# A long convolution's inverse transform: u times D added in PSUM by an identity matmul, the odd classes' second sums on GpSimd, and one rotation pass for both halves

## The chip, the core and the metric

The kernel runs on one core of a Trainium2 chip. The core has a matrix engine (TensorE, PE in the rows; PEld is its weight load), a vector engine (VectorE, DVE), a scalar engine (ScalarE, ACT), GpSimd (POOL) and a queue engine (SyncE, SP) that here only issues DMAs. Each engine works through a queue of its own in order; semaphores make one wait for another. The metric is device time in microseconds, the median of several runs.

## The reference, cut to what matters

Two independent parts are computed and joined along the last axis. Part A is attention over 64 segments of 32 tokens, with eight memory tokens carried from each segment to the next, so that segments follow one another. Part B is a state-space layer: a convolution kernel K of length 2048 per channel from 128 complex states, applied to u (2048 x 1024) by an FFT of length 4096, and u times a vector D added:

```python
P = jnp.exp(logdA[:, :, None] * l[None, None, :])
K = jnp.einsum('dn,dnl,dn->dl', Cc, P, dB).real
...
Yf = Uf * Kf[None, :, :, :]
y = irfft2(Yf, ...).astype(jnp.bfloat16)[:, :, 0, :L]
y = transpose(y, 0, 2, 1) + u * Dskip[None, None, :]
```

## The kernel before

The program runs part B first, then part A. Part B (`part_b`, from L709) has two stages. The first, up to about 400 us, builds the tables and transforms u; it leaves the transform of u in DRAM (`Ud`, f32), the rows that give the spectrum of K, and the matrices of the inverse transform (`MId`). The second, which the change edits, is called the Transform here: the loop `for b in range(16)` at L1547 and the tail behind it.

The loop's iteration b is one of four blocks of frequencies (`kc = b % 4`) of one of four quarters of the channels (`dq = b // 4`, 256 channels each). A block has two halves (`n_`), each with two sub-blocks and a real and an imaginary part: 128 x 1024 numbers in f32. Within an iteration:

- PE forms the spectrum of K for iteration b + 1 (`spectrum`, L1214, products at L1221, 20 for each half) into PSUM (`hps`, three buffers; `pa` in the first iterations).
- DVE multiplies it by the transform of u (`times_u`, L1374): `Z` and `Y` at L1377, one operand in SBUF (`wq`, the loaded `Ud`), one in PSUM. `rotate` (L1379) makes a complex product of them in two half-size passes, L1380 and L1381. The first half is rotated before the second half's products; the second half after the u work of the iteration.
- `pointwise` (L1443) then adds and subtracts the halves on DVE: the sum (`even`, tile `ev`, f32) at L1456, the difference straight into the bf16 operand `Bt[:, kc, 1]` at L1457. GpSimd makes the even classes' two second sums from `even` (L1459, 512 wide each). There is no second sum for the odd classes.
- From iteration 4 on, PE computes two inverse products (`inverses(2)`) for the quarter that was finished before. An output block is a pair of row blocks c of class r = c // 4; the eight pairs are taken in the order `PAIRS = (0, 4, 2, 6, 8, 12, 10, 14)`, so that each iteration has one even and one odd class. `products_back` (L1500, products at L1511) runs over two row blocks, four kc and two parts: 16 products for an even class; for an odd class 32, as it reads both sub-blocks of the difference, the second through matrices whose sign ACT has turned (`negated`, L1470, tile `mn`, L1474). Some pairs get one more small product (L1506).
- ACT scales the result out of PSUM into bf16 (`yb`, L1526). `ending` (L1530) multiplies the u rows by D on DVE (L1531) and adds `yb` (L1532); the write to DRAM is issued on ACT's queue (L1533). These endings are run by `end()` in the next iteration, between the second half's products and its rotation.

SP's queue carries everything that is loaded, in an order that the program fixes: in each iteration the two halves of `Ud` for the next one (L1212, each waits until DVE has used the old one), then between none and three weight blocks for part A of 512 KB (`residents`, L1682; the load is L268), each into a place that part B has given up, and then the u rows for later inverse products (`load_inverse`, L1464, three ahead, seven buffers `uu`). Iteration 6 also loads the second set of K's rows (L1095), on which the spectrum of iteration 8 depends.

After the loop three inverse products of the last quarter are begun in the `hps` banks (`begun`, L1603) with the first three kc, and the last eight inverses run, with nine weight loads after the first and one after each other. Then part A starts: DVE copies the first kept weights through PSUM into `arena` (L335), PE runs the projections (L414) and the output products (L527), and weights that don't fit are streamed again in every segment (`wst`).

Of the kernel before, what the change touches and what calls it, by code (L numbers as in the profile page):

```python
# [708 lines left out]
def part_b(ctx, tc, u, A_re, A_im, B_re, B_im, C_re, C_im, log_dt, Dskip, out_b, ahead, copies, residents, first_state):  # L709
# [732 lines left out]

    def pointwise(b, s_):  # L1443
        kc, Bt = b % 4, Bs[b // 4]
        Y = first
        if b:
            Y = pw.tile([128, 2, 2, 2, DQ], F32, name="y", tag="y")[:]
            for n_ in range(2):
                Z = pw.tile([128, 2, 2, DQ], F32, name="z", tag="z")[:]
                times_u(s_, Y[:, n_], Z, n_)  # L1450
                if n_ == 0:
                    rotate(Y[:, n_], Z)
        yield
        if b:
            rotate(Y[:, 1], Z)
        v.tensor_tensor(out=even[:], in0=Y[:, 0], in1=Y[:, 1], op=ALU.add)  # L1456
        v.tensor_tensor(out=Bt[:, kc, 1], in0=Y[:, 0], in1=Y[:, 1], op=ALU.subtract)  # L1457
        for i, op in ((0, ALU.add), (1, ALU.subtract)):
            gp.tensor_tensor(out=Bt[:, kc, 0, i], in0=even[:, 0], in1=even[:, 1], op=op)  # L1459

    NIV, UU = 3, 7
    unsent = []

    def load_inverse(dq, c):  # L1464
        r, mc = c // 4, c % 4
        uu = iv.tile([128, 2, DQ], BF16, name="uu", tag="uu", bufs=UU)
        sy.dma_start(out=uu[:], in_=u_v[r][:, mc:mc + 2, DQ * dq:DQ * dq + DQ])
        return uu

    def negated(c):  # L1470
        cs, mn = (None, 1, None, 0)[c // 4], None
        if cs is not None:
            mn = mnp.tile([128, 2, 4, 128], BF16, name="mn", tag="mn")
            sc.activation(out=mn[:], in_=MI[c // 2][:, :, cs], func=ACT.Copy, scale=-1.0)  # L1474
        return cs, mn

    ready = []

    def inverses(n):

        for _ in range(n):
            dq, c = todo.pop(0)
            if not ready:
                ready.append(negated(c))
            inverse(dq, c, nxt.pop(0), *ready.pop(0))
            if len(todo) >= NIV:
                nxt.append(load_inverse(*todo[NIV - 1]))
# [3 lines left out]
    def prepare(n):  # L1491
        while len(ready) < min(n, len(todo)):
            ready.append(negated(todo[len(ready)][1]))

    def inverse_begin(dq, c, yp):
        prepare(3)
        early[dq, c] = yp
        products_back(yp, dq, c, *ready[PAIRS.index(c)], range(3))

    def products_back(yp, dq, c, neg, mn, kcs):  # L1500
        r, Bt = c // 4, Bs[dq]
        j = r % 2
        for b in range(2):
            for kc in kcs:
                if kc == 3 and b == 1 and c % 4 == 2:
                    pe.matmul(yp[:, b, :], lhsT=l4[:, r, :], rhs=w4[:, DQ * dq:DQ * dq + DQ], start=False, stop=False, skip_group_check=True)  # L1506
                for cs in range(2):
                    hs = (0, 1) if j else (r // 2,)
                    for half in hs:
                        lhs = mn[:, b] if j and half and cs == neg else MI[c // 2][:, b, cs]  # L1510
                        pe.matmul(yp[:, b, :], lhsT=lhs[:, kc, :], rhs=Bt[:, kc, j, half, 1 - cs if j and half else cs, :],  # L1511
                                  start=(b == 0 and kc == 0 and cs == 0 and half == hs[0]), stop=(kc == 3 and cs == 1 and half == hs[-1]),
                                  skip_group_check=True)

    def inverse(dq, c, uu, neg, mn):
        r, mc = c // 4, c % 4
        d = slice(DQ * dq, DQ * dq + DQ)
        if (dq, c) in early:
            yp = early[dq, c]
            products_back(yp, dq, c, neg, mn, range(3, 4))  # L1520
        else:
            yp = ps_y.tile([128, 2, DQ], F32, name="yp", tag="yp")[:]
            products_back(yp, dq, c, neg, mn, range(4))
        prepare(2)
        yb = iv.tile([128, 2, DQ], BF16, name="yb", tag="yb", bufs=2)
# [3 lines left out]

        def ending():  # L1530
# [246 lines left out]
```

## Time and profile before

| What | Value |
|---|---|
| median of three runs | 1961.17 us (1948.34, 1961.17, 1962.83) |
| profiled execution, its own time | 1945.78 us |
| span of the profiled execution | 1944.1 us |
| mean granted TensorE clock | 0.976 |
| loop of the Transform, first product of iteration 4 to that of iteration 15 | 446.35 to 575.22 us |
| first product of part A on PE | 607.84 us |

A row of a timeline has the start and the length in us, the engine, the line, the operation, the tile written and the tiles read, shapes (partitions x elements) and a count of merged instructions; a bracket at its end gives how long the engine had stood idle and what ended the wait. Adjacent rows of one engine overlap a little, so the pitch from start to start is the cost of one. A row of windows gives a stretch, then its length, the busy time of PE, PEld, DVE, ACT and POOL with the number of instructions, the granted clock, the share of time that the DMA engines were busy, and GB/s. A row of waits gives who waited for whom: the total, the number of times and the longest.

### The profile page before, as it was taken

How to read it: one execution, taken by the hardware profiler on the slowest of the kernel's cores; microseconds unless marked ns; L12 is line 12 of the kernel's file. 1: busy time of each engine (PE TensorE's matmuls, PEld its weight loads, DVE VectorE, ACT ScalarE, POOL GpSimd, SP SyncE). 2: the span in 40 equal slices, each digit the busy share in tenths (PEclk: the TensorE clock that was granted, in tenths of full speed). 3: DMA queues.
4: the chain of work that ended last, by engine and by line, in shares of the span. 5: the costliest groups of instructions: out<-in, count | busy, mean ns of one | idle time of the engine just before them, and what ended most of it. 6: DMA issues, size and time to landing. Idle time of an engine off the chain costs nothing.

```text
span 1944.1 us, 74320 instructions
## 1 busy us (share of the span) xinstructions
PE 1802.1 (93%) x31750; PEld 1115.6 (57%) x31788; DVE 1370.7 (71%) x3431; ACT 935.6 (48%) x1670; POOL 459.2 (24%) x855
## 2 busy tenths in 40 slices
PE   8999999887997899998999999999999999999998
PEld 3666566556775455555555555555555555555554
DVE  8699999789893566666676666666666666666650
ACT  8799999851112344443444444444434443434330
POOL 2363545223222111111121111111111111111120
PEclk9999999869998999999999999999999999999999
DMA  7889898867589999999999999999999999999990
GB/s 223 248 237 270 253 285 244 217 190 254 169 264 322 349 337 349 348 350 321 349 349 345 346 347 345 344 340 348 339 333 357 352 343 342 340 345 353 342 348 27
DMA packets 337343, 591.09 MB, mean 304 GB/s; under 512 B 94848, under 2 KB 211048, under 8 KB 334964
## 3 DMA queue, kind: packets, MB, share of 16 engines
q1 hardware_dynamic: 284824, 531.85, 80.2%
q10 hardware_dynamic: 45532, 29.57, 5.0%
q0 software_dynamic: 6656, 24.92, 3.5%
q8 instruction: 249, 4.08, 0.8%
q14 instruction: 82, 0.67, 0.1%
HBM read 528.78 MB, written 68.47 MB: 307 GB/s over the span
## 4 chain that ended last, share of the span: by engine, by line
PE 39%; DMA 27%; DVE 2%; ACT 1%; issue 1%; SPq 0%; POOL 0%; ACTq 0%; POOLq 0%; DVEq 0%
PE acc L414 22%; DMA wst<-WD_v 11%; DMA wst<-WD_o 9%; PE pp L527 9%; PE pe L664 3%; PE tr L425 2%; DMA wst<-WD_k 2%; DMA arena<-PKd 2%; PE pv L495 1%; DMA wst<-WD_q 1%; DMA out_dram<-arena 1%; DVE arena L621 1%; PE pv L499 1%; ACT arena L621 1%; DMA out_dram<-uu 1%
## 5 line engine op out<-in xcount | busy, mean ns | idle before, releaser
L414 PEld LDWEIGHTS <-a_hT 128*32 128x32 bf16 x12352 | 329.4, 96 | 324.0 <-issue 64.6
L420 ACT CAST arena<-acc 128x512 bf16<-128x512 f32 x384 | 225.1, 586 | 389.5 <-PE acc L414 316.3
L414 PE MATMUL acc<-wst,a_hT 128*32 128x512 bf16 x2304 | 230.4, 383 | 33.0 <-DMA wst<-WD_v 26.1
L527 PEld LDWEIGHTS <-arena 128*32 128x32 bf16 x8256 | 216.2, 97 | 77.0 <-issue 53.0
L428 POOL COPY arena<-arena 128x128 bf16<-128x128 bf16 x128 | 37.4, 292 | 697.3 <-PE tr L425 352.4
L335 DVE TENSOR_SCALAR arena<-keep 128x256 int32<-128x256 int32 (+1 forms) x512 | 175.6, 395 | 27.7 <-PE acc L414 27.5
L414 PE MATMUL acc<-XM,a_hT 128*32 128x512 bf16 x2560 | 173.0, 381 | 0.0
L454 DVE TENSOR_REDUCE a_mx<-sc 128x4 f32<-128x160 f32 (+1 forms) x192 | 71.8, 374 | 74.0 <-PE sc L442 74.0
L197 PE MATMUL pro<-XM,wsl 128*128 128x512 bf16 x480 | 117.7, 382 | 5.4 <-DVE kst L206 2.2
L527 PE MATMUL pp<-W_o,arena 128*32 128x256 bf16 x3584 | 120.7, 273 | 0.4 <-issue 0.4
L414 PE MATMUL acc<-W,a_hT 128*32 128x512 bf16 x1536 | 119.7, 384 | 0.0
L542 DVE COPY arena<-tr 128x512 bf16<-128x512 bf16 x64 | 27.2, 425 | 127.1 <-PE tr L425 127.1
L458 ACT ACTIVATE sc<-sc 128x160 f32<-128x160 f32 (+1 forms) x192 | 63.9, 333 | 105.1 <-DVE sc L455 104.8
L462 DVE TENSOR_REDUCE a_mx<-sc 128x4 f32<-128x160 f32 (+1 forms) x192 | 72.8, 379 | 55.3 <-ACT sc L458 55.1
L489 POOL TENSOR_TENSOR arena<-arena,a_BD 128x128 bf16<-128x128 bf16 x128 | 51.0, 399 | 218.0 <-DVE arena L472 213.2
L1266 DVE TENSOR_SCALAR nr<-ptt 128x456 f32<-128x456 int16 x128 | 80.4, 628 | 30.5 <-PE ptt L1244 27.5
L1258 ACT ACTIVATE E<-pa 128x648 bf16<-128x648 f32 x128 | 87.6, 712 | 17.1 <-PE pa L1250 15.5
L527 PE MATMUL pp<-wst,arena 128*32 128x256 bf16 x1536 | 76.4, 274 | 17.6 <-DMA wst<-WD_o 16.7
L414 PE MATMUL acc<-wq,a_hT 128*32 128x512 bf16 x1024 | 92.4, 383 | 0.0
L513 ACT CAST arena<-pv 128x512 bf16<-128x512 f32 (+1 forms) x128 | 61.3, 479 | 63.5 <-PE pv L499 33.1
L1459 POOL TENSOR_TENSOR Bt<-ev 128x512 bf16<-128x512 f32 x32 | 55.7, 1762 | 151.5 <-DVE ev L1456 151.5
L414 PE MATMUL acc<-g,a_hT 128*32 128x512 bf16 x1024 | 90.9, 381 | 0.0
(339 smaller groups left out, 4023.9 us busy)
## 6 DMA issues: line engine op xcount, KB each, us to landing
wst<-WD_v SPq DMA_DIRECT2D x256, 512.0 KB
wst<-WD_k SPq DMA_DIRECT2D x192, 512.0 KB
wst<-WD_o SPq DMA_DIRECT2D x192, 512.0 KB
wst<-WD_q SPq DMA_DIRECT2D x128, 512.0 KB
Ud<-ux POOLq DMA_DIRECT2D x16, 1024.0 KB, 8.4
wq<-Ud SPq DMA_DIRECT2D x32, 512.0 KB
wsl<-in_A_Wk_dram SPq DMA_DIRECT2D x16, 512.0 KB
wsl<-in_A_Wv_dram SPq DMA_DIRECT2D x16, 512.0 KB
```

The source lines that it names most:

```text
L197: nc.tensor.matmul(a[:], lhsT=w[:, kc, 128 * j:128 * j + 128], rhs=xTl[:, kc, :, :].rearrange("p s k -> p (s k)"), start=(kc == 0), stop=( ...
L335: nc.vector.tensor_scalar(out=out.bitcast(I32), in0=in_.bitcast(I32), scalar1=0, scalar2=None, op0=ALU.bitwise_or)
L414: nc.tensor.matmul(a[32 * g:32 * g + 32, o_:o_ + rhs.shape[1]], lhsT=hT[:, kc, :], rhs=rhs, start=(kc == 0), stop=(kc == KC - 1), tile_pos ...
L420: nc.scalar.copy(out=q, in_=a[:])
L454: nc.vector.tensor_reduce(out=m_, in_=x, axis=AX.X, op=ALU.max)
L458: nc.scalar.activation(out=flat(sc, i), in_=flat(sc, i), func=ACT.Exp, scale=scale)
L462: nc.vector.tensor_reduce(out=m_, in_=x, axis=AX.X, op=ALU.add)
L513: copy(out=o[:, i:i + n], in_=p[:, i:i + n, :].rearrange("p a (g q) -> p a g q", g=4))
L527: nc.tensor.matmul(po[32 * qt:32 * qt + 32, o_:o_ + rhs.shape[1]], lhsT=oT[:, h % 4, (h % 16) // 4, :], rhs=rhs, start=False, stop=(h == 3 ...
L664: nc.tensor.matmul(pe[n][:], lhsT=left[2 * b + hi // 16][:, 128 * (hi % 16):128 * (hi % 16) + 128], rhs=wo[u][:, 1024 * hh + 512 * n:1024 ...
L1258: sc.activation(out=T["E", r, e // 4][:, lo:lo + 8 * NE].rearrange("p (i c) -> p i c", i=2), in_=T.pop(("p", r, e))[:, :, 0:4 * NE], func= ...
L1266: v.tensor_scalar(out=T["n", r, e // 4][:, lo:lo + 8 * NT], in0=T.pop(("t", r, e))[:, 0:8 * NT].bitcast(I16)[:, 0:16 * NT:2], scalar1=floa ...
```

## The change

`Y` and `Z` become one tile each for both halves (`Yp`, `Zs`), and `even` is laid into the second half of `Zs`. From iteration 4 on both halves are rotated together, after the iteration's u work, in two passes of 128 x 1024; before that each half is rotated alone, as it was. The difference is written in f32 (`odd`), and GpSimd makes from it the two second sums of the odd classes, reading one operand with its halves in reversed order; in iteration 15 DVE makes these two. So an odd class needs 16 products, as an even one, and the negated matrices go, with ACT's work on them. The u rows are loaded in pairs into one tile (three buffers of two); one DVE pass (`skips`) multiplies a pair by D, before the inverse product that needs it, and PE adds the rows to the sum in PSUM with an identity matrix that has been scaled once by PLEN / 2 (a matmul of 512 columns per inverse). ACT's scaled copy `yb` (three buffers, two before) is then the result itself, written from there; the write of one inverse is issued after the copy of the next, no longer after a DVE sum.

```diff
-    mnp = ctx.enter_context(tc.tile_pool(name="b_mn", bufs=2))
     evp = ctx.enter_context(tc.tile_pool(name="b_ev", bufs=1))
-    even = evp.tile([128, 2, 2, DQ], F32, name="ev")
+    odd = evp.tile([128, 2, 2, DQ], F32, name="od")
...
+    Zs = pw.tile([128, 2, 2, 2, DQ], F32, name="z")
+    Yp = pw.tile([128, 2, 2, 2, DQ], F32, name="y")
+    even = Zs[:, 1]
+
+    def blocks(t_):
+        return t_.rearrange("p i c d -> p (i c) d")
+
     def pointwise(b, s_):
         kc, Bt = b % 4, Bs[b // 4]
-        Y = first
+        Y = Yp[:] if b else first
+        whole = b > 3
         if b:
-            Y = pw.tile([128, 2, 2, 2, DQ], F32, name="y", tag="y")[:]
             for n_ in range(2):
-                Z = pw.tile([128, 2, 2, DQ], F32, name="z", tag="z")[:]
-                times_u(s_, Y[:, n_], Z, n_)
-                if n_ == 0:
-                    rotate(Y[:, n_], Z)
+                times_u(s_, Y[:, n_], Zs[:, n_], n_)
+                if n_ == 0 and not whole:
+                    rotate(Y[:, n_], Zs[:, n_])
         yield
-        if b:
-            rotate(Y[:, 1], Z)
-        v.tensor_tensor(out=even[:], in0=Y[:, 0], in1=Y[:, 1], op=ALU.add)
-        v.tensor_tensor(out=Bt[:, kc, 1], in0=Y[:, 0], in1=Y[:, 1], op=ALU.subtract)
+        if whole:
+            rotate(Y.rearrange("p n a c d -> p (n a) c d"), Zs[:].rearrange("p n a c d -> p (n a) c d"))
+        elif b:
+            rotate(Y[:, 1], Zs[:, 1])
+        v.tensor_tensor(out=even, in0=Y[:, 0], in1=Y[:, 1], op=ALU.add)
+        v.tensor_tensor(out=odd[:], in0=Y[:, 0], in1=Y[:, 1], op=ALU.subtract)
         for i, op in ((0, ALU.add), (1, ALU.subtract)):
             gp.tensor_tensor(out=Bt[:, kc, 0, i], in0=even[:, 0], in1=even[:, 1], op=op)
-
-    NIV, UU = 3, 7
+        eng, to = v if b == 15 else gp, blocks(Bt[:, kc, 1])
+        eng.tensor_tensor(out=to[:, 0:4:3], in0=odd[:, 0], in1=odd[:, 1, ::-1], op=ALU.add)
+        eng.tensor_tensor(out=to[:, 2:0:-1], in0=odd[:, 0], in1=odd[:, 1, ::-1], op=ALU.subtract)
...
     def load_inverse(dq, c):
         r, mc = c // 4, c % 4
-        uu = iv.tile([128, 2, DQ], BF16, name="uu", tag="uu", bufs=UU)
-        sy.dma_start(out=uu[:], in_=u_v[r][:, mc:mc + 2, DQ * dq:DQ * dq + DQ])
+        i = turn_of[0] % 2
+        turn_of[0] += 1
+        if i == 0:
+            pairs.append(iv.tile([128, 2, 2, DQ], BF16, name="uu", tag="uu", bufs=3))
+        uu = pairs[-1][:, i]
+        sy.dma_start(out=uu, in_=u_v[r][:, mc:mc + 2, DQ * dq:DQ * dq + DQ])
         return uu
...
+    def skips():
+        dq = todo[0][0]
+        uu = pairs.pop(0)
+        d = slice(DQ * dq, DQ * dq + DQ)
+        uu = uu[:].rearrange("p i a d -> p (i a) d")
+        v.tensor_tensor(out=uu, in0=uu, in1=Dsk[:, d].unsqueeze(1).to_broadcast([128, 4, DQ]), op=ALU.mult)
...
                 for cs in range(2):
-                    hs = (0, 1) if j else (r // 2,)
-                    for half in hs:
-                        lhs = mn[:, b] if j and half and cs == neg else MI[c // 2][:, b, cs]
-                        pe.matmul(yp[:, b, :], lhsT=lhs[:, kc, :], rhs=Bt[:, kc, j, half, 1 - cs if j and half else cs, :],
...
+                    pe.matmul(yp[:, b, :], lhsT=MI[c // 2][:, b, cs, kc, :], rhs=Bt[:, kc, r % 2, r // 2, cs, :],
+                              start=(b == 0 and kc == 0 and cs == 0), stop=False, skip_group_check=True)
...
-        prepare(2)
-        yb = iv.tile([128, 2, DQ], BF16, name="yb", tag="yb", bufs=2)
+        pe.matmul(yp.rearrange("p b d -> p (b d)"), lhsT=ident[:], rhs=uu.rearrange("p b d -> p (b d)"), start=False, stop=True, skip_group_check=True)
+        yb = iv.tile([128, 2, DQ], BF16, name="yb", tag="yb", bufs=3)
         sc.activation(out=yb[:], in_=yp, func=ACT.Copy, scale=float(2.0 / PLEN))
         while unsent:
             unsent.pop(0)()
-
-        def ending():
-            v.tensor_tensor(out=uu[:], in0=uu[:], in1=Dsk[:, d].unsqueeze(1).to_broadcast([128, 2, DQ]), op=ALU.mult)
-            v.tensor_tensor(out=uu[:], in0=uu[:], in1=yb[:], op=ALU.add)
-            unsent.append(lambda: sc.dma_start(out=out_v[r][:, mc:mc + 2, d], in_=uu[:]))
-        endings.append(ending)
+        unsent.append(lambda: sc.dma_start(out=out_v[r][:, mc:mc + 2, d], in_=yb[:]))
...
         next(points)
-        end()
+        if b >= 4:
+            skips()
...
     for n_ in range(8):
+        if n_ % 2 == 0:
+            skips()
         inverses(1)
```

More of the change, by code (lines that the diff above doesn't have):

```diff
@@ L1482, in inverses @@
             dq, c = todo.pop(0)
-            if not ready:
-                ready.append(negated(c))
-            inverse(dq, c, nxt.pop(0), *ready.pop(0))
+            inverse(dq, c, nxt.pop(0))
             if len(todo) >= NIV:
```

34 lines of the change are left out of this document (8 added, 26 removed).

## The prediction

> **What bounds the kernel now.** I read the page first, for where the time lies, then the timeline of the stage that the change edits.
>
> ```profile
> span 1944.1 us, 74320 instructions
> ...
> PE 1802.1 (93%) x31750; PEld 1115.6 (57%) x31788; DVE 1370.7 (71%) x3431; ACT 935.6 (48%) x1670; POOL 459.2 (24%) x855
> ...
> PE acc L414 22%; DMA wst<-WD_v 11%; DMA wst<-WD_o 9%; PE pp L527 9%; PE pe L664 3%; PE tr L425 2%; DMA wst<-WD_k 2%; DMA arena<-PKd 2%; PE pv L495 1%; DMA wst<-WD_q 1%; DMA out_dram<-arena 1%; DVE arena L621 1%; PE pv L499 1%; ACT arena L621 1%; DMA out_dram<-uu 1%
> ```
>
> The chain that ended last is nearly all part A (L414, L527, streamed weights), which the change leaves alone. So the edit can only move the moment at which part A starts. Two windows over the Transform follow (columns: length, busy time of PE, PEld, DVE, ACT, POOL, granted clock, DMA share, GB/s), then one iteration of its loop on the vector engine (DVE).
>
> ```profile
> 501.00:585.00 84.00, 78.64 (x704) 67.16 (x704) 79.47 (x104) 18.43 (x25) 24.12 (x15) 1.00 0.69 212
> ...
> 540.00:560.00 20.00, 19.68 (x178) 16.85 (x176) 19.23 (x25) 4.47 (x6) 6.72 (x4) 1.00 0.92 281
> ```
> ```profile
> 561.51 1.23 DVE L1456 TENSOR_TENSOR ev<-y 128x1024 f32<-128x1024 f32 x1
> 562.65 1.22 DVE L1457 TENSOR_TENSOR Bt<-y 128x1024 bf16<-128x1024 f32 x1
> 563.79 1.22 DVE L1377 TENSOR_TENSOR z<-wq,hps 128x1024 f32<-128x1024 f32 x1
> 564.92 1.22 DVE L1377 TENSOR_TENSOR y<-wq,hps 128x1024 f32<-128x1024 f32 x1
> 566.17 0.69 DVE L1380 TENSOR_TENSOR y<-y,z 128x512 f32<-128x512 f32 x1
> 566.78 0.69 DVE L1381 TENSOR_TENSOR y<-y,z 128x512 f32<-128x512 f32 x1
> 567.55 1.22 DVE L1377 TENSOR_TENSOR z<-wq,hps 128x1024 f32<-128x1024 f32 x1
> 568.69 1.21 DVE L1377 TENSOR_TENSOR y<-wq,hps 128x1024 f32<-128x1024 f32 x1
> 569.82 0.42 DVE L1531 TENSOR_TENSOR uu<-uu,Dsk 128x512 bf16<-128x512 bf16 x1
> 570.35 0.43 DVE L1532 TENSOR_TENSOR uu<-uu,yb 128x512 bf16<-128x512 bf16 x1
> 570.69 0.42 DVE L1531 TENSOR_TENSOR uu<-uu,Dsk 128x512 bf16<-128x512 bf16 x1
> 571.21 0.42 DVE L1532 TENSOR_TENSOR uu<-uu,yb 128x512 bf16<-128x512 bf16 x1
> 571.55 0.69 DVE L1380 TENSOR_TENSOR y<-y,z 128x512 f32<-128x512 f32 x1
> 572.15 0.69 DVE L1381 TENSOR_TENSOR y<-y,z 128x512 f32<-128x512 f32 x1
> 572.94 1.23 DVE L1456 TENSOR_TENSOR ev<-y 128x1024 f32<-128x1024 f32 x1
> ```
>
> No row has a bracket: DVE never waits, and an iteration takes 572.94 - 561.51 = 11.43 us. PE is nearly as busy, but follows: it waits for DVE's products. So here DVE sets the pace.
>
> **The change, part by part.** I price by pitch (start to start), since rows overlap by about 0.08.
>
> DVE, iterations 4 to 15. The u work, two L1531 and two L1532, fills 569.82 to 571.55, 1.73 us. It becomes one product of twice the width: 0.34 for 512 (570.35 to 570.69 for the same form) gives about 0.6. The four rotations (0.61 each, and 0.11 to 0.18 of waiting for a result where one follows another) become two of 1024 at 1.14, with one such wait of 0.17. Before: 11.43. After: even 1.14, odd 1.14, four products 4.54, u 0.6, rotations 1.14 + 1.31: 9.87, before new waits. The odd difference in f32 instead of bf16 costs the same: L1456 and L1457 have the same pitch.
>
> POOL and the new wait. Two sums per iteration become four.
>
> ```profile
> 562.81 2.19 POOL L1459 TENSOR_TENSOR Bt<-ev 128x512 bf16<-128x512 f32 x1 [8.02 <-DVE ev L1456]
> ```
> ```profile
> 562.81 3.41 POOL L1459 TENSOR_TENSOR Bt<-ev 128x512 bf16<-128x512 f32 x2 [8.02 <-DVE ev L1456]
> ...
> 586.65 1.49 DVE L1531 TENSOR_TENSOR uu<-uu,Dsk 128x512 bf16<-128x512 bf16 x1
> ...
> 585.68 3.58 POOL L1459 TENSOR_TENSOR Bt<-ev 128x512 bf16<-128x512 f32 x2 [8.01 <-DVE ev L1456]
> ```
>
> The first sum takes 2.19 because L1457 runs beside it; the second 1.26. The other way round, L1531 takes 1.49 instead of 0.42 while POOL sums (586.65). Operations of the two engines that read two SBUF tensors exclude each other, for a whole instruction. The products with hps (PSUM) run beside POOL unhurt (563.79, 564.92: 1.22).
> `even` now lies in the second Z buffer, so the second half's Z product must wait until POOL has read it. Counted from the start of `even`: POOL's second sum ends at 566.23 - 561.51 = 4.72; that product would be due at 1.14 + 1.14 + 2 x 1.13 = 4.54. With signalling I take a wait of 0.25. Queued behind it on DVE is all the rest. The third and fourth sums end at 4.72 + 2 x 1.23 = 7.2, and the u product is due at 4.8 + 2.27 = 7.07: it waits about 0.1. The odd sums read one operand in reversed order of halves, which no row has; ends: 1.26 as now (they then hide), or twice that, when the u product and a rotation each wait for one sum, about +2.5 per iteration. I take 1.26, as the element count and types are the same row's. So an iteration becomes 9.87 + 0.35 = 10.22, a saving of 1.2.
>
> PE and ACT. Per iteration 16 products go (the odd class reads one block per matrix, no longer two), two identity matmuls of 512 columns come.
>
> ```profile
> 501.56 4.53 PE L1221 MATMUL hps<-k,XM 128*128 128x256 bf16 x40
> ...
> 536.61 1.69 PE L1511 MATMUL yp<-Bt,MI 128*128 128x256 bf16 x14
> ...
> 584.64 0.28 PE L1511 MATMUL hps<-Bt,mn 128*128 128x256 bf16 x1 [3.34 <-ACT mn L1474]
> ...
> 585.76 0.85 PE L1511 MATMUL hps<-Bt,MI 128*128 128x256 bf16 x3
> ```
>
> 40 products are 4.53, so 0.11 each: 4.5 + 32 x 0.11 + two identities (0.22 to 0.4 each) = 8.6 to 8.9 us against 10.2: hidden while DVE sets the pace. ACT's 16 negations (`mn`) go; they held the path only at 584.64. PE now idles 1.4 us more per iteration.
>
> Iterations 0 to 3. DVE keeps its half-size rotations, and two more POOL sums of 1.26 now collide with the first half's rotations.
>
> ```profile
> 415.15 0.96 DVE L1205 TENSOR_TENSOR XM<-XM,wq 128x1536 bf16<-128x1536 bf16 x1 [0.85 <-ACT wq L1196]
> ...
> 427.56 1.22 DVE L1377 TENSOR_TENSOR z<-wq,pa 128x1024 f32<-128x1024 f32 x1 [2.25 <-PE pa L1221]
> ...
> 480.31 1.22 DVE L1377 TENSOR_TENSOR z<-wq,hps 128x1024 f32<-128x1024 f32 x1 [1.09 <-DMA wq<-Ud]
> ...
> 493.70 1.22 DVE L1377 TENSOR_TENSOR z<-wq,hps 128x1024 f32<-128x1024 f32 x1 [1.87 <-PE hps L1221]
> ...
> 486.86 0.39 PE L1221 MATMUL hps<-k,g 128*128 128x256 bf16 x1 [8.91 <-DMA k<-Kx]
> ...
> 477.31 3.87 SPq L1095 DMA_DIRECT2D k<-Kx x3
> ...
> SPq L1467 <- DMA out_dram<-uu: 10.6, 1, 10.6
> ```
>
> Each of three iterations can lose up to two sums, 2.5 us; the idle 0.85 and 2.25 give most of the first two back. I take +2.4 by iteration 4 (ends 0 and 7.5).
> Iteration 8 starts (493.70) when PE has its first product, which waited 8.9 us for the k rows, which SP issued at 477.31, behind iteration 6's load. Iterations 4 to 6 save about 2.0 together (the fourth had no u work before and loses 0.4) and first pay back the 2.4. But SP had stood 10.6 us for a write-back's landing ahead of a u load (last row; window 462 to 478), and write-backs now go out earlier, no longer waiting for DVE's sum. I take 2.0 gained at iteration 8 (ends: 4.5, or -1 if that stand stays and the u product waits for it, which now holds up all of DVE).
> Iterations 8 to 15:
>
> ```profile
> 575.22 1.22 DVE L1377 TENSOR_TENSOR z<-wq,hps 128x1024 f32<-128x1024 f32 x1
> ...
> 609.70 0.43 DVE L1531 TENSOR_TENSOR uu<-uu,Dsk 128x512 bf16<-128x512 bf16 x1 [11.46 <-DMA uu<-in_B_u_dram]
> ...
> 616.39 1.40 PE L414 MATMUL acc<-arena,a_hT 128*32 128x512 bf16 x4 [6.86 <-DVE arena L335]
> ...
> 623.92 0.61 PE L414 MATMUL acc<-a_half,a_hT 128*32 128x512 bf16 x2 [3.60 <-DMA a_half<-in_A_Wq_dram]
> ...
> 591.06 10.37 DMA out_dram<-uu
> ```
>
> From 493.70 to 575.22 (start of iteration 15) is 81.5 us; 7 x 10.22 = 71.5, plus 2 for loads that land later: with weights in flight the DMA share is 0.92 (window 540 to 560), and the same bytes now come in 10% less time. That leaves 8.0 gained.
>
> The tail, from iteration 15 to part A. Here the trace shows DVE waiting 11.46 us for u rows queued behind weights. Those loads keep their places among SP's, so they land as long after iteration 15 as now. What gets worse: the last identity needs the last u product, so PE can begin part A only after it, and the last inverse (16 products, 1.8 us) and the first quads come behind; PE now waits there anyway (616.39), and again at 623.92. The write-back now reads `yb`, three buffers; a write took 10.37 (last row), so ACT waits for landings. I take +1.0 (ends -4, if weights start sooner, and +6).
>
> Sum: -2.0 - 8.0 + 1.0 = -9.0. The profiled execution took 1945.78 (span 1944.1), so 1936.8 by its own measure; it lies 15.4 below the median of the runs, 1961.17 (1948.34 to 1962.83). On the median: 1952.2.
>
> **The rivals.**
> 1. Hidden: weights and part A's first segment, not DVE, set the start. For it: share 0.92 and the 3.60 at 623.92. Against: 0.69 over 501 to 585, so there is room, and the weights wait for buffers that the loop frees. Of the 9.0 about 2 are left: 1959.
> 2. u rows late, the slower side. DVE's queue is in order, and its u product stands ahead of rotations and sums. If rows take about 10 us, as the write at 591.06, a load issued some 7 us into an iteration (SP first waits for the second half's y product, done at 6.0) lands at 17, against a need at 15.0 (10.2 + 4.8): 2 us per iteration. It decides from 1.2 per iteration on; at 3.5, with the rows behind three weights, 11 x 2.3 = 25 less the 2.0 at iteration 8 and with the tail's 1: 1985. Against: the loop's present u products have no wait in the rows above.
> 3. PE's clock. After the idle of 3.34 us at 584.64 three products take 0.85 instead of about 0.4 (3/14 of 1.69): half clock. At half clock PE needs 17 us per iteration, not 8.6, and would set the pace; a lapse as long as that idle, 3.4 us, costs 1.7, so one per iteration takes 11 x 1.7 = 19, of which PE's slack of 1.4 hides 15: about 1957. I expect idle stretches under 2 us. The Trainium skill (TensorE: Matmul & The Clock Gate, Part 1) says that an idle window of about 3.4 us halves the clock; by that rule the loop stays at full speed, and only PE's wait for iteration 15's u product could trip it; the trace agrees at 584.64.
> 4. More: iteration 8 gains 4.5, no late loads (2 more), and the tail 4 instead of losing 1: 4.5 + 10 + 4 = 18.5, so 1942.7.
>
> **How the numbers follow.** Chances: forecast 0.53 (its own range 1946 to 1957), hidden 0.18, late rows 0.11, clock 0.07, more 0.11. Range 1940 to 1964: the 'more' case less some scatter below, the hidden case with the runs' own 1962.83 above; only late rows and half of the clock's tail lie outside. One per cent, about what a measurement of this kernel can tell, is 19.6 us. Faster by more needs the 'more' case or half of it with the runs' 14 us scatter: 0.14. Slower: half of late rows, 0.06. The same: 0.80.
>
> **What would show it.** Right: between two `even` rows 10.2 us; one u product of 0.67; a bracket of about 0.25 on the second Z product, from POOL; four POOL sums, the last three about 1.26; no `mn`; part A's arena quads some 9 us before 616.39. Wrong: a bracket from DMA on the u product inside the loop, a u product of over 1.5 (POOL's odd sums slow), PE below clock 1.00 between iterations 8 and 14, or quads that start earlier while the segment after ends where it did.

## The result, and the profile after

| | median | ratio to before |
|---|---|---|
| before | 1954.88 us (1946.18 to 1968.59, 22 runs) | |
| changed | 1948.59 us (1938.83 to 1956.89, 22 runs) | 0.9968, 95% interval 0.9954 to 0.9982 |

The change saves 6.3 us (3.5 to 9.0 by the interval). The kernel before has here a median that lies, by chance, also 6.3 us below that of the three runs which the prediction started from.

The page of the changed kernel, its first rows, and the two windows that were shown of before:

```profile
span 1945.7 us, 73775 instructions
...
PE 1787.6 (92%) x31526; PEld 1092.0 (56%) x31564; DVE 1357.6 (70%) x3362; ACT 918.6 (47%) x1654; POOL 496.5 (26%) x885
```
```profile
501.00:585.00 84.00, 74.33 (x615) 59.87 (x613) 80.27 (x74) 10.15 (x17) 48.42 (x38) 0.94 0.74 230
540.00:560.00 20.00, 16.93 (x131) 13.09 (x130) 18.31 (x17) 1.79 (x3) 10.12 (x8) 0.91 0.92 284
```

The engines' work fell as the change says (PE 14.5 us, DVE 13.1, ACT 17.0 less; GpSimd 37.3 more), yet the span of this one execution is 1.6 us longer. The second window has DVE at 18.31 of 20: before it was 19.23. DVE now waits. Both readings need the pace and the waits apart. First the pace, an iteration with one short wait, on DVE and then on GpSimd:

```profile
505.91 1.23 DVE L1463 TENSOR_TENSOR z<-y 128x1024 f32<-128x1024 f32 x1
507.05 1.22 DVE L1464 TENSOR_TENSOR od<-y 128x1024 f32<-128x1024 f32 x1
508.19 1.21 DVE L1377 TENSOR_TENSOR z<-wq,hps 128x1024 f32<-128x1024 f32 x1
509.32 1.21 DVE L1377 TENSOR_TENSOR y<-wq,hps 128x1024 f32<-128x1024 f32 x1
510.66 1.22 DVE L1377 TENSOR_TENSOR z<-wq,hps 128x1024 f32<-128x1024 f32 x1
511.80 1.21 DVE L1377 TENSOR_TENSOR y<-wq,hps 128x1024 f32<-128x1024 f32 x1
512.93 0.72 DVE L1489 TENSOR_TENSOR uu<-uu,Dsk 128x1024 bf16<-128x1024 bf16 x1
513.57 1.21 DVE L1380 TENSOR_TENSOR y<-y,z 128x1024 f32<-128x1024 f32 x1
514.70 1.21 DVE L1381 TENSOR_TENSOR y<-y,z 128x1024 f32<-128x1024 f32 x1
515.95 1.23 DVE L1463 TENSOR_TENSOR z<-y 128x1024 f32<-128x1024 f32 x1
```
```profile
507.28 3.35 POOL L1466 TENSOR_TENSOR Bt<-z 128x512 bf16<-128x512 f32 x2 [4.22 <-DVE z L1463]
510.59 1.27 POOL L1468 TENSOR_TENSOR Bt<-od 128x512 bf16<-128x512 f32 x1
511.83 1.27 POOL L1469 TENSOR_TENSOR Bt<-od 128x512 bf16<-128x512 f32 x1
```

From one even sum to the next are 515.95 - 505.91 = 10.04 us, where before had 11.43. The wait for GpSimd's read of `even` is the 0.2 between 510.45 (one pitch of 1.13 behind 509.32) and 510.66. GpSimd's sums end at 513.10, just after the u product starts at 512.93: it takes 0.72 instead of 0.69.

Then the waits of DVE's u product, all of them in this execution:

```profile
469.47 0.69 DVE L1489 TENSOR_TENSOR uu<-uu,Dsk 128x1024 bf16<-128x1024 bf16 x1 [4.09 <-DMA uu<-in_B_u_dram]
492.85 0.69 DVE L1489 TENSOR_TENSOR uu<-uu,Dsk 128x1024 bf16<-128x1024 bf16 x1 [3.25 <-DMA uu<-in_B_u_dram]
...
544.31 0.69 DVE L1489 TENSOR_TENSOR uu<-uu,Dsk 128x1024 bf16<-128x1024 bf16 x1 [1.02 <-DMA uu<-in_B_u_dram]
554.74 0.69 DVE L1489 TENSOR_TENSOR uu<-uu,Dsk 128x1024 bf16<-128x1024 bf16 x1 [0.33 <-DMA uu<-in_B_u_dram]
576.09 0.69 DVE L1489 TENSOR_TENSOR uu<-uu,Dsk 128x1024 bf16<-128x1024 bf16 x1 [1.21 <-DMA uu<-in_B_u_dram]
604.06 0.69 DVE L1489 TENSOR_TENSOR uu<-uu,Dsk 128x1024 bf16<-128x1024 bf16 x1 [18.05 <-DMA uu<-in_B_u_dram]
609.28 0.69 DVE L1489 TENSOR_TENSOR uu<-uu,Dsk 128x1024 bf16<-128x1024 bf16 x1 [4.53 <-DMA uu<-in_B_u_dram]
```

Five stand in the loop, 9.9 us together, two in the tail. In the tail PE waits behind them, and then part A for what follows:

```profile
604.81 0.58 PE L1524 MATMUL yp<-uu,b_ident 128*128 128x512 bf16 x1 [7.08 <-DVE uu L1489]
...
615.54 1.25 PE L414 MATMUL acc<-arena,a_hT 128*32 128x512 bf16 x4 [2.33 <-DVE arena L335]
622.84 0.61 PE L414 MATMUL acc<-a_half,a_hT 128*32 128x512 bf16 x2 [4.49 <-DMA a_half<-in_A_Wq_dram]
```

To compare executions I count from iteration 0's first even sum, the last point ahead of the changed code (it lies between 405.5 and 408.8 us in all fourteen profiles, without order). The columns are starts: the first product of iterations 4, 8 and 15 on DVE, and the two stretches of part A's first segment on PE that the prediction named ("quads": the projections that read `arena`, then those that read `a_half`).

| kernel | it. 4 | it. 8 | it. 15 | arena quads | a_half quads | ratio to before (95%) |
|---|---|---|---|---|---|---|
| before | 40.9 | 88.2 | 169.8 | 210.9 | 218.5 | |
| changed | 42.0 | 89.6 | 161.6 | 207.0 | 214.3 | 0.9968 (0.9954 to 0.9982) |
| e1 rows asked for earlier | 42.3 | 87.3 | 157.5 | 200.0 | 207.4 | 0.9953 (0.9935 to 0.9971) |
| e2 and in the tail | 42.3 | 89.5 | 160.2 | 201.0 | 209.8 | 0.9928 (0.9903 to 0.9953) |
| e3 and five yb | 43.9 | 90.1 | 161.2 | 193.9 | 208.2 | 0.9926 (0.9903 to 0.9950) |
| e4 rotations alone | 42.8 | 86.4 | 167.4 | 207.6 | 215.7 | 0.9974 (0.9953 to 0.9996) |
| e5 u product later | 42.0 | 86.3 | 156.7 | 203.7 | 211.4 | 0.9946 (0.9928 to 0.9964) |
| e6 identity alone | 43.0 | 92.1 | 169.5 | 217.3 | 224.8 | 1.0011 (0.9989 to 1.0033) |
| e7 odd sums alone | 42.3 | 91.0 | 179.6 | 220.4 | 228.1 | 1.0070 (1.0045 to 1.0095) |
| e8 four weights later | 42.1 | 85.0 | 156.2 | 201.5 | 205.7 | 0.9966 (0.9945 to 0.9987) |
| e9 all of e3 and e5 | 42.4 | 87.9 | 158.0 | 196.9 | 207.6 | 0.9934 (0.9910 to 0.9957) |
| e10 and whole from the start | 42.4 | 87.1 | 157.2 | 195.7 | 207.2 | 0.9931 (0.9900 to 0.9962) |
| e11 four weights later, one load kept | 42.0 | 87.3 | 157.5 | 195.2 | 201.3 | 0.9931 (0.9906 to 0.9956) |
| e12 e1 and five yb | 42.4 | 86.5 | 157.3 | 200.4 | 207.5 | 0.9951 (0.9932 to 0.9970) |

What is left of a profiled execution behind the a_half quads is 1319 to 1330 us long in all rows but e8's (1337). That scatter of one execution hides a shift of a few us in its span: the changed kernel's span is 1.6 us longer although its first segment starts 4.1 us earlier by this count, because iteration 0's even sum came 3.1 us later in its execution and what follows the quads took 2.7 us more. The ratios are over many runs.

The milestones are one execution each, and they scatter too. e1, e2, e3, e8, e11 and e12 run the same program up to the end of the loop, yet iteration 8 starts at 85.0 to 90.1 and iteration 15 at 156.2 to 161.2. e3, e9 and e10 have the same tail, and their arena quads come 32.7 to 38.8 us behind iteration 15. So a difference of up to 5 or 6 us at one milestone counts only where the waits in front of it account for it.

### The profile page after: what moved, and what is told of

It reads as the page before. It is cut to its first block, busy times and chain, and to the rows that moved or that the text cites. A ratio compares the mean times of both kernels' runs of the same rounds, so it can differ in the third digit from the quotient of the medians.

```text
span 1945.7 us, 73775 instructions
## 1 busy us (share of the span) xinstructions
PE 1787.6 (92%) x31526; PEld 1092.0 (56%) x31564; DVE 1357.6 (70%) x3362; ACT 918.6 (47%) x1654; POOL 496.5 (26%) x885
## 4 chain that ended last, share of the span: by engine, by line
PE 45%; DMA 32%; DVE 13%; ACT 6%; issue 3%; POOL 1%; SPq 0%; ACTq 0%; DVEq 0%; POOLq 0%
PE acc L414 20%; DMA wst<-WD_v 11%; DMA wst<-WD_o 9%; PE pp L527 7%; DMA wst<-WD_k 3%; PE pe L664 3%; DMA arena<-PKd 3%; PE tr L425 2%; PE pro L184 2%; DMA out_dram<-arena 2%; PE pro L197 1%; DMA uu<-in_B_u_dram 1%; DVE nr L1266 1%; DMA out_dram<-yb 1%; DMA wst<-WD_q 1%
## 5 line engine op out<-in xcount | busy, mean ns | idle before, releaser
L425 PEld LDWEIGHTS <-arena 128*128 128x128 bf16 x1024 | 57.9, 98 | 59.6 <-ACT arena L420 28.6
```

The costliest lines, as they stand in the source:

```text
L425: nc.tensor.transpose(out=p[:, hl, :, :].rearrange("p a b -> p (a b)"), in_=q[:, 128 * hl:128 * hl + 128], identity=ident[:])
```

## The experiments

Theory A: the loop became as fast as forecast, and u rows that land late, behind a DVE queue in order, gave part of it back. Theory B: weights and part A's first segment set its start, so that DVE's waits cost nothing. Theory C: GpSimd's sums, or other late data, eat the gain.

**e1: rows asked for one block earlier.**

```diff
-    NIV = 3
+    NIV = 4
```

> The changed kernel with each pair of u rows asked for one block of outputs earlier (NIV 4 for 3), nothing else. Theory A (the loop became as fast as forecast, and late u rows in DVE's in-order queue gave much of it back): the brackets from DMA on the u product in iterations 5 and 7 (4.1 and 3.3 us in the changed kernel) shrink under 0.5 each, iteration 8 starts at about 82 to 84 us after iteration 0's even sum, in place of 89.6, and about two thirds of that, 4 to 5 us, reaches part A and the time: ratio to before about 0.9945. Theory B (weights and the first segment of part A set its start whatever the loop does): the brackets go too, but the arena quads stay about 207 us after iteration 0's even sum and the time is that of the changed kernel, ratio 0.9968 within 0.001. Theory C (GpSimd's extra sums are what eats the gain, and the DMA brackets only stand where DVE would wait anyway): the time lost moves to brackets from POOL, and iteration 8 stays at 88 us or more.

Rows of DVE that wait in the loop, and the two in the tail:

```profile
473.37 1.22 DVE L1377 TENSOR_TENSOR z<-wq,hps 128x1024 f32<-128x1024 f32 x1 [2.38 <-DMA wq<-Ud]
...
495.77 1.22 DVE L1377 TENSOR_TENSOR z<-wq,hps 128x1024 f32<-128x1024 f32 x1 [2.06 <-DMA wq<-Ud]
596.75 0.69 DVE L1489 TENSOR_TENSOR uu<-uu,Dsk 128x1024 bf16<-128x1024 bf16 x1 [16.10 <-issue]
602.25 0.69 DVE L1489 TENSOR_TENSOR uu<-uu,Dsk 128x1024 bf16<-128x1024 bf16 x1 [4.81 <-DMA uu<-in_B_u_dram]
```

No u product waits in the loop, so 8.7 us of brackets ahead of iteration 15 are gone. But the `Ud` rows of iterations 6 and 8, on the same queue, are late next, 4.8 us in all with a bracket of 0.34: other late data, so C holds for that much, while no bracket over 0.25 us is GpSimd's. Iteration 8 comes 2.3 us earlier, not 6 to 8, iteration 15 gains 4.0 and the quads 7. In e2 and e3, whose loop is the same, the `Ud` rows of iteration 6 are later still:

```profile
474.96 1.22 DVE L1377 TENSOR_TENSOR z<-wq,hps 128x1024 f32<-128x1024 f32 x1 [5.68 <-DMA wq<-Ud]
```
```profile
475.35 1.22 DVE L1377 TENSOR_TENSOR z<-wq,hps 128x1024 f32<-128x1024 f32 x1 [3.93 <-DMA wq<-Ud]
```

Their iteration 8 stands at 89.5 and 90.1, where the changed kernel's is. So the edit takes the u waits away, but what reaches iteration 15 varies, 0.4 to 5.4 us in the six executions with this loop. That the quads moved speaks against B in its plain form; the time doesn't decide, since the ratios of e1 and of the changed kernel overlap.

**e5: the same rows, the product later.** In `pointwise`, behind `rotate`:

```diff
+        if b >= 4:
+            skips()
         v.tensor_tensor(out=even, in0=Y[:, 0], in1=Y[:, 1], op=ALU.add)
...
         next(points)
-        if b >= 4:
-            skips()
```

> The changed kernel with the product u times D moved in DVE's order: behind the two rotations and ahead of the even sum, about 2.4 us later in the iteration; the loads of the u rows are untouched. Theory A (the cost is the product's place in an in-order queue ahead of the rotations): the DMA brackets of 4.09 and 3.25 us in iterations 5 and 7 shrink to about 1.7 and 0.9, those of about 1 us in iterations 12 to 14 go, an iteration stays at 10.0 to 10.1, iteration 15 starts 155 to 157 us after iteration 0's even sum (changed kernel 161.6) and the time falls by 2 to 5 us, ratio about 0.995; the tail's waits stay. Theory B (start of part A set elsewhere): the loop gains the same and the arena quads don't move, ratio 0.997. Theory C (DVE waits for something else that comes late, the Ud rows or PE): the brackets move to the next product of the next iteration with their full length, iteration 15 stays at 160 or more.

```profile
467.22 0.69 DVE L1491 TENSOR_TENSOR uu<-uu,Dsk 128x1024 bf16<-128x1024 bf16 x1 [2.17 <-DMA uu<-in_B_u_dram]
...
488.85 0.69 DVE L1491 TENSOR_TENSOR uu<-uu,Dsk 128x1024 bf16<-128x1024 bf16 x1 [1.30 <-DMA uu<-in_B_u_dram]
```

4.09 and 3.25 became 2.17 and 1.30, the later ones are gone, iteration 15 is at 156.7, and the ratio 0.9946: near A's numbers, though the interval overlaps the changed kernel's. With no load moved, the place of the waiting product in the queue alone was worth 4.9 us at iteration 15, and the brackets that shrank or went account for it (5.2 us, less the 0.35 below). C's waits don't appear: in the iterations after, the longest other bracket is 0.35, for `Ud` in iteration 6.

**e2 and e3: the tail.** Both with e1's edit. e2 issues the last loads of u rows ahead of the nine weights, the last pair into a buffer of its own in memory that the loop has left; e3 also gives the fourth and fifth of the tail's `yb` buffers there.

```diff
     ctx2.close()
+    tailp = ctx.enter_context(tc.tile_pool(name="b_tail", bufs=1))
+    while len(nxt) < len(todo):
+        nxt.append(load_inverse(*todo[len(nxt)], tailp if len(nxt) > 5 else None))
...
+        yb = tailp.tile([128, 2, DQ], BF16, name="yt%d" % len(todo)) if tailp and len(todo) in (3, 4) else iv.tile(...)
```

> The kernel of e1 with the last loads of u rows issued at the loop's end, ahead of the nine weights, the last pair into a buffer of its own. Theory A: the waits of 18.05 and 4.53 us on the u products of the tail go, so do the two PE waits for them and the half clock behind them; what is left is the write landings that yb's three buffers wait for. The arena quads come 3 to 5 us earlier than in e1 and the time falls by 2 to 4 us more, ratio about 0.993. Theory B: the quads don't move by over 1 us, because the weights that they read or the first state set them; time as e1.

> The kernel of e2 with five buffers for yb in the tail instead of three. Theory A: the ACT waits of 7.4, 2.1 and 3.0 us for write landings at least halve, and the arena quads come another 1 to 4 us earlier, ratio about 0.992. If the buffers are hidden behind something else (PSUM, weights), the waits go and the quads stay: time as e2.

PE in the tail of e2, then of e3:

```profile
593.43 3.20 PE L1512 MATMUL yp<-Bt,MI 128*128 128x256 bf16 x16 [5.25 <-ACT yb L1526]
607.80 1.40 PE L414 MATMUL acc<-arena,a_hT 128*32 128x512 bf16 x4 [4.76 <-DVE arena L335]
616.59 0.61 PE L414 MATMUL acc<-a_half,a_hT 128*32 128x512 bf16 x2 [4.30 <-DMA a_half<-in_A_Wq_dram]
```
```profile
592.23 1.91 PE L1512 MATMUL yp<-Bt,MI 128*128 128x256 bf16 x16 [2.52 <-ACT yt L1526]
601.24 1.25 PE L414 MATMUL acc<-arena,a_hT 128*32 128x512 bf16 x4 [0.70 <-DVE arena L335]
615.47 0.61 PE L414 MATMUL acc<-a_half,a_hT 128*32 128x512 bf16 x2 [11.42 <-DMA a_half<-in_A_Wq_dram]
```

In e2 the waits of 18.05 and 4.53 are gone (0.48 is left), but PE then waits 5.25 for ACT, whose `yb` waits for writes to land (4.19, 2.11, 2.01, 2.01 and 4.20 us for the last five copies). The arena quads stand 1.0 us later than in e1, where A had them 3 to 5 earlier: a miss. Counted from iteration 15, as the loops came out unequal, it is 40.8 us to them, 42.5 in e1, 45.5 in the changed kernel (47.0 in e5, whose tail is the changed kernel's). With five buffers it is 32.7, but PE then stands 11.42 us for a_half (7.96 in e9, 8.69 in e10), and those quads stay at 208. There B holds: once DVE, PE and ACT are out of the way, the first segment's own load sets the pace. Of the 8 us between e2 and e3 at this place nothing measurable reaches the time.

**e12: five yb without the earlier loads.** e1 with the line for `yb` of e3 alone.

> The kernel of e1 with e3's five yb buffers in the tail, the late loads of u rows left behind the nine weights. It tells apart what the tail's delay consists of. Theory A (u rows, product, identity, yb and landing are one chain, and the first link that is late sets it): the u waits of about 16 and 5 us stay, the yb buffers alone bring nothing, arena quads 41 to 43 us after iteration 15 as in e1 (42.5), ratio 0.9953 within 0.002. Rival (the yb landings are the main link): the quads come 4 us or more earlier than in e1, 38 or less after iteration 15, ratio as e3, 0.993.

Of DVE and PE in its tail:

```profile
594.52 0.69 DVE L1489 TENSOR_TENSOR uu<-uu,Dsk 128x1024 bf16<-128x1024 bf16 x1 [16.24 <-issue]
```
```profile
595.26 0.59 PE L1524 MATMUL yp<-uu,b_ident 128*128 128x512 bf16 x1 [4.96 <-DVE uu L1489]
```

From iteration 15 to the arena quads it is 43.1 us, as in e1 (42.5): the buffers alone bring nothing. The loads alone bring 1.7 (e2), which is inside the scatter, and both bring 4 to 10 (e3 32.7; e9 and e10 with the same tail 38.8 and 38.6; e11 37.7). That fits one chain, as A says, as far as one execution of each can tell.

**e8 and e11: the a_half load earlier.** e3 with four of the last eight weights left for part A to ask for later:

```diff
-LATE = 8
+LATE = 4
...
-                load_resident(tc, wres, src, k_, W_res)
+                load_resident(tc, wres, src, k_, W_res, None, places.pop(0)() if places else None)
```

In e8 this lets another load slip forward, a weight into the place of the small rows that the products at L1510 read: the last two inverses wait for it (8.99 us on PE) and read the weight instead of their rows. In e11 four yields ahead of that load keep it where it was.

> The kernel of e3 with four of the eight last weights left for part A to ask for, so that the first segment's own loads (the half of Q's block and its companions) come ahead of them. Theory A with its limit: after e3 the first segment waits 11.4 us on PE for a_half, which was asked for behind eight weights of 512 KB; at the 400 GB/s of that stretch four of them are 5.2 us, so the a_half quads come 4 to 6 us earlier (from 208.2 to 202 to 204 us after iteration 0's even sum) and the time falls by 2 to 5 us against e3, unless the four weights are then late in the segment's second half. Theory B in its strong form (all bytes of the first segments must land, in whatever order): the quads move and the time does not.

> As e8, but the one load that e8 let slip forward (a weight into the place of the fourth-order rows, on which PE's last inverses then waited 8.99 us) stays at the end as in e3. Theory B for the tail (a_half, asked for behind the last weights, holds the first segment): the 8.99 goes, the a_half quads come 3 to 6 us earlier than e3's relative to iteration 15 (41 to 44 us after it instead of 47.0). If the time then falls below e3's, the order of the loads was the last link; if the four postponed weights are missed in the same segment, the waits for streamed weights behind the a_half quads grow by as much (from 0.9 and 5.2 to 9 together or more) and the time is e3's, ratio 0.992 to 0.995.

e8 missed its forecast: the a_half quads came at 205.7, not 202 to 204, and the time is above e3's. It says nothing on the order of the loads, as its wait of 8.99 is of its own making. PE in e11:

```profile
609.69 0.39 PE L414 MATMUL acc<-a_half,a_hT 128*32 128x512 bf16 x2 [3.22 <-DMA a_half<-in_A_Wq_dram]
...
634.59 0.40 PE L527 MATMUL pp<-W_o,arena 128*32 128x256 bf16 x8 [0.49 <-DMA W_o<-in_A_Wo_dram]
635.95 0.62 PE L527 MATMUL pp<-W_o,arena 128*32 128x256 bf16 x16 [0.95 <-DMA W_o<-in_A_Wo_dram]
```

The a_half quads come 43.8 us after iteration 15 (foreseen 41 to 44), 3.2 us closer to it than in e3; by the table they are 6.9 earlier, of which 3.7 lie in the loop, where the two programs are the same. The two waits for streamed weights behind them are as in e3 (0.93 and 5.25; 0.90 and 5.21), so the postponed weights aren't missed there; but the output products of the segment now wait for theirs. With the streamed weights beside them PE's waits between the second and the third segment add up to 4.0 us, and e3 has none over 0.4 there. The first score products (L442) of the first three segments start 206.3, 217.5 and 238.6 us after iteration 0's even sum; in e3 212.7, 223.8 and 239.9. So 6.4 us became 1.3 within two segments, and the ratio is e3's. That is what B's strong form foresees for this stretch: the bytes have to land, in whatever order.

**e4, e6, e7: one part of the change at a time, on the kernel before.** e4 has `Zs`, `Yp`, `even` in `Zs` and `whole` as in the diff of the change, nothing else. e6 has the pairs of u rows, `skips`, the identity matmul and three `yb`; negated matrices and the 32 products stay. e7 has `odd` with GpSimd's two more sums, and 16 products; `ending` stays.

> The kernel before with one part of the change alone: Z's two halves in one buffer, even written into its second half, and from iteration 4 on one rotation pass over both halves; u products, second sums and negations as before. By the prediction's terms an iteration loses 4 x 0.61 plus 0.4 of waits and gains 1.14 + 1.31: about -0.4 us, plus up to 0.25 of stall on the second Z product, so 11.43 becomes 11.0 to 11.3; over iterations 8 to 15 that is -1 to -3 us and over the whole loop -2 to -5. Theory A: 1 to 3 us of that reach the time, ratio about 0.999. Theory C (the new wait for GpSimd's read of even costs as much as the merge saves): iteration time 11.4 or more, ratio 1.000 or above.

> The kernel before with the identity matmul alone: u times D in one pass per two blocks, added in PSUM, yb written out; half rotations, odd classes with negated matrices and two products per block stay. By the prediction's terms the u work falls from 1.73 to 0.6 us, so an iteration from 11.43 to 10.3; PE, with 16 more products than in the changed kernel, needs 1.76 + 8.6 to 8.9 = about 10.5 and so becomes the pace, or shares it. Theory A: 10.3 to 10.6 per iteration in the clean ones, late u rows give back 5 to 10 us in iterations 5, 7 and in the tail as in the changed kernel, ratio 0.997 to 0.999. Theory B: ratio 1.000 within 0.001, since part A starts where it did.

> The kernel before with the odd sums alone: odd in f32, four GpSimd sums per iteration, one block per matrix on PE, no negations; u work and half rotations as before. DVE saves nothing by this part, PE 1.8 us per iteration which it had to spare. GpSimd's four sums end 7.2 us after even starts, and the first half's two rotations stand at 4.7 to 6.0 in that time: by the exclusion seen before, each waits for a sum. Theory A: an iteration takes 12.0 to 13.5 instead of 11.43 and the kernel is slower than before by 5 to 15 us, ratio 1.002 to 1.008; with the merged rotations, which come after 7.2, this cost is gone, so that the parts of the change need each other. Rival: the sums only delay GpSimd itself, an iteration stays at 11.4, ratio 0.999 to 1.000.

Rows of DVE in e6, then in e7, from one even sum to the next:

```profile
472.62 0.69 DVE L1479 TENSOR_TENSOR uu<-uu,Dsk 128x1024 bf16<-128x1024 bf16 x1 [4.52 <-DMA uu<-in_B_u_dram]
...
563.56 0.69 DVE L1479 TENSOR_TENSOR uu<-uu,Dsk 128x1024 bf16<-128x1024 bf16 x1 [3.43 <-DMA uu<-in_B_u_dram]
```
```profile
548.44 1.23 DVE L1456 TENSOR_TENSOR ev<-y 128x1024 f32<-128x1024 f32 x1
...
553.09 0.69 DVE L1380 TENSOR_TENSOR y<-y,z 128x512 f32<-128x512 f32 x1
553.70 1.75 DVE L1381 TENSOR_TENSOR y<-y,z 128x512 f32<-128x512 f32 x1
...
560.93 1.22 DVE L1456 TENSOR_TENSOR ev<-y 128x1024 f32<-128x1024 f32 x1
```

e4 takes 11.15 per iteration, as its terms say; its ratio 0.9974 is below the 0.999 that I expected, which its interval just takes in. e6 takes 10.30: DVE stays the pace, not PE as I had thought possible. But the loop gains nothing by iteration 15 (169.5), as the waits for u rows in iterations 5, 7 and 13 (4.52, 3.12, 3.43) eat it, and the tail is 7 us longer than before's: 1.0011, no change. My expectation of 0.997 to 0.999 missed; B's value was right for another reason than B's, as the quads didn't stay but came 6 us later. e7 takes 560.93 - 548.44 = 12.49, because the second rotation waits for a sum (1.75 instead of 0.69), and is slower, 1.0070. The three ratios add up to +0.55% where the whole change has -0.32%. In the loop's clean iterations, -0.28, -1.13 and +1.06 add up to -0.35 us, and the whole has -1.39: the merged rotations lie behind GpSimd's last sum, so together the collision of e7 vanishes.

**e9 and e10: together.** e9 is e3 with e5's later product; e10 has the one pass of rotations from iteration 1 on as well.

```diff
-        whole = b > 3
+        whole = b > 0
```

> The kernel of e3 (rows a block earlier, tail loads ahead of the nine weights, five yb in the tail) with the later place of the u product of e5. Theory A: the in-loop waits for u rows are gone already in e3, so the later place adds nothing there beyond 0.5 us; what varies is the wait of iterations 5 and 7 for Ud rows (2 to 6 us in e1 to e3, 0.4 to 1.3 in e5 and e8). Iteration 15 at 156 to 160 us after iteration 0's even sum, arena quads at 192 to 197, a_half quads at 206 to 209 where DMA holds them; time as e3 within 0.002, ratio 0.991 to 0.993. If the place mattered by itself (another work for DVE while rows are late), it is below 0.990.

> The kernel of e9 with the one pass of rotations in iterations 1 to 3 too, where the half rotations collide with GpSimd's odd sums (1.75 instead of 0.69 us, once per iteration). Theory C in its small form: iteration 4 starts 2 to 3 us earlier relative to iteration 0's even sum (about 39.5 instead of 42.0), and the time falls by 1 to 3 us against e9. Rival: in these iterations DVE waits for PE and for ACT anyway (brackets of 0.8 to 2.4 on the next products), so that the 1.06 per iteration were hidden: iteration 4 at 41.5 to 42.5 and the time as e9; and the one pass, which can't start before the second half's products, may push the even sum back by up to 0.6 per iteration.

DVE in e10, iterations 1 to 3:

```profile
428.77 1.22 DVE L1377 TENSOR_TENSOR z<-wq,pa 128x1024 f32<-128x1024 f32 x1 [2.78 <-issue]
442.27 1.22 DVE L1377 TENSOR_TENSOR z<-wq,pa 128x1024 f32<-128x1024 f32 x1 [1.42 <-POOL Bt L1471]
```

e9 is e3 again, 1939.6 us, 0.9934. In e10 iteration 4 starts at 42.4, as in e9: the early collisions were hidden (the wait at 428.77 is 0.65 in e9), and the wait for GpSimd's read of `even` is 1.42 here. The rival was right. e2, e3, e9, e10 and e11 can't be told apart by time; they are the fastest, 0.7% below before, and e2 is the shortest edit of them; e2's and e3's intervals end just below where the changed kernel's begins (0.9953 and 0.9950 against 0.9954), the others' overlap it by less than 0.001. The intervals of e1, e5 and e12 overlap those of the five.

## Why the prediction was right, and which steps were not

The forecast, 1952.2 on a median of 1961.17, meant -9.0 us; -6.3 came (interval -9.0 to -3.5). The median, 1948.59, lies 3.6 below the forecast because the kernel before came out 6.3 lower. By the milestones of one execution the terms are +1.4 at iteration 8, -9.6 from there to 15, +4.3 in the tail, -3.9 together. The sign and the mechanism, a shorter DVE iteration, are right, and the size is right within a third; but two terms were too good and one too bad, and that they partly cancel is luck. Point by point:

- **The iteration, 11.43 to 10.22.** Right in each row, 10.04 measured: the wait for `even`'s read is 0.2 (taken 0.25), the u product's delay 0.03 (taken 0.1). The odd sums with a reversed operand take 1.27 (taken 1.26; the other end of 2.5 per iteration is out).
- **Iterations 0 to 3, +2.4.** Too much: 42.0 - 40.9 = +1.1. The collisions are there, in each of the three iterations, but DVE has waits there anyway (1.42 in the last row): e10, without the collisions, starts iteration 4 no earlier.

```profile
413.77 1.75 DVE L1381 TENSOR_TENSOR y<-y,z 128x512 f32<-128x512 f32 x1
...
427.10 1.76 DVE L1381 TENSOR_TENSOR y<-y,z 128x512 f32<-128x512 f32 x1
...
430.27 1.22 DVE L1377 TENSOR_TENSOR z<-wq,pa 128x1024 f32<-128x1024 f32 x1 [1.42 <-issue]
```

- **Iteration 8 starts 2.0 earlier.** This step failed: in the profiled execution it starts 1.4 later (89.6 against 88.2). Its bad end, -1 "if that stand stays and the u product waits for it", is what happened. SP's stand for a write's landing is shorter but there, and about half of it passes before ACT issues that write (461.31 us); the waits of SP from 462 to 478 us:

```profile
SPq L1084 <- DMA out_dram<-yb: 6.1, 1, 6.1
```

  Behind it stand the rows for iteration 5's product, which waited 4.09; those of iteration 7 came 3.25 late. e5 gives back 3.3 us at this milestone by its shorter brackets. e1 gives back 2.3, but e2 and e3 with the same loop nothing, as the `Ud` rows are late instead. So late rows held the loop here, u rows first, as rival 2 has it, but only in two iterations with full size, where the K rows and weights stand in the same queue, and not in all eleven.
- **Iterations 8 to 15, -8.0.** -9.6 measured (81.5 to 71.9). The 2 us of late loads were 1.02 and 0.33 before iteration 15, and the iteration was 0.18 shorter.
- **The tail, +1.0.** This step failed in size: from iteration 15 to the arena quads it is +4.3, to the a_half quads +4.1 (e5, with the same tail, is 1.6 and 2.0 us longer still). The reason given, that u loads keep their places and PE waits anyway, overlooked that now DVE, PE, ACT and the write-back are in one chain: u rows, product, identity, `yb`, landing. And part A doesn't begin only after the last identity: PE ran its first products at 596.04 us, in the wait ahead of 604.81; what comes behind the last inverses are the arena quads. Against e1, mending the first link (e2) brings the quads 1.7 us closer to iteration 15 and mending the last (e12) puts them 0.6 further off, both within the scatter; both together bring 4 to 10, and then a_half holds PE, and behind it (e11) the bytes of the weights. That one chain is the cause is argued from these single executions; the time tells it from the changed kernel's only just (e2, e3).
- **The rivals.** Hidden is wrong for the first 3 to 7 us beyond the changed kernel at the a_half quads (e5 and e1) and right further on: e1, e2, e3, e9, e10 and e12 all stand at 207 to 210 there, and e11, which gets to 201, loses it again. PE's clock fell a little, 0.94 in the window of the loop, but the iterations from 8 on kept 10.04 to 10.06 (one 10.18) wherever the rows were there.
- **The signs.** Those of being right came, but for the arena quads, which are 3.9 us earlier and not 9. Two signs of being wrong came as well: DMA brackets on the u product in the loop, 9.9 us in all, and a PE clock below 1.00 between iterations 8 and 14, which left the pace as it was. The third, quads that start earlier while the next segment ends where it did, didn't come: the first score products (L442) of the first three segments start 4.2, 4.3 and 5.1 us earlier than before's, counted from iteration 0's even sum, and e1's a further 6.9, 7.1 and 6.8.

## What to carry to other kernels

An operation that waits for a DMA, moved ahead of other work in an engine's in-order queue, is priced by the landing of its data in the crowded stretch (here 7.3 us in two iterations); ask for the data earlier, or place the operation behind the work that doesn't need it. Parts of one change may need each other: the second sums alone cost 0.7%, and here the merged rotations make room for them. In a chain of waits that cover each other one mended link shows little: mend two before dropping either, and look whether plain bytes come next.

## What the runs showed of the hardware

- **PE's clock after a wait.** Sixteen products that follow a wait of 5.25 us take 3.20 (e2), after 2.52 us 1.91 (e3): a rate little above half at a granted clock of 0.55, and the full one at 1.00. The Trainium skill (TensorE: Matmul & The Clock Gate, Part 1) has the clock fall after an idle window of about 3.4 us, which lies between. But the loop of the changed kernel has a wait of 2.41 us with slow products behind it:

```profile
551.98 3.22 PE L1221 MATMUL hps<-k,XM 128*128 128x256 bf16 x20 [2.41 <-DVE y L1377]
```

  Twenty products take 2.35 at the full clock, and the window from 552.0 to 555.2 has 0.70 granted. So a lower clock can follow a wait below 3.4 us too; what decides it isn't shown.
- **A DVE rotation waits out a GpSimd sum.** The first half's second rotation takes 1.75 us beside one in e7, in every iteration, against 0.69 alone.
- **Small loads behind large ones.** Rows of 128 KB took 2.2 to 2.6 us to land when issued ahead of the weights (e3, 578 to 584 us), and 8 to 9 us behind three of 512 KB (the changed kernel, issued at 566.85 and 568.49, landed at 576.07 and 576.44). The DMAs of SP and ACT share eight semaphores in the trace, and each issue waits for the landing of the transfer that had its semaphore before: so a write-back of ACT's can hold up SP, the 6.1 us above.
